# A fused attention and two-MLP kernel: the hidden layer of the first MLP's later part by Strassen's seven block products

## The chip, the cores and the metric

One core of one Trainium2 chip runs the whole program. The metric is the device time of one execution in microseconds (us); the median of several executions counts. The kernel before takes 798.88 us (median of 3 runs, 798.6 to 800.25).

## What is computed

The reference, cut to what matters (attention is left out: it yields x of 2304 tokens and 512 features):

```python
def _moe_ref(x, w_in, w_out, s, b):      # x 2304x512, w_in 512x2048, w_out 2048x512
    h = x @ w_in
    r = np.maximum(h, 0.0)
    g = s * (r * r) + b
    return (g @ w_out).astype(np.float32)

def _moe2_ref(x, w_in, w_out, g_ln):     # w_in 512x1024, w_out 1024x512
    h = x @ w_in
    ...                                  # softmax(h) * h, layer norm, gain g_ln
    return (ln @ w_out).astype(np.float32)
```

The inputs are float64, the result is float32, and all products need nearly float32 accuracy.

## The kernel before, in words

**Products in three terms.** Each operand of the MLPs is split into a high and a low part (F32R, the single-pass float32 form of TensorE). A product is high x high, high x low and low x high, three matmuls into one accumulator in PSUM. In the first MLP the weights are the stationary tile (128 x 128) and the tokens are the moving columns, up to 512 at a time (`NB`); in the second MLP the tokens are stationary.

**Weights.** `order` (line 392) lists all weight tiles: `("in", f)` and `("out", f)` for the 16 chunks of 128 hidden features, then `in2` and `out2` of the second MLP. `decode(n)` (line 441) fetches one as float64 words by a DMA on SP's queue (`fetch`, line 421: 512 KB into one of three `raw` buffers), makes float32 of it with one ScalarE and four VectorE instructions (lines 432 to 438), and splits it into high and low (lines 459, 460). `wpA` and `wpB` hold 28 tiles, and a new one takes the place of an old one. `decode_to` is called from the loops below and so sets how early a tile is made. For `in2`, which is already multiplied by Strassen's scheme, four combinations of blocks are formed on GpSimd (line 451).

**Stages.** Attention (to about 260 us) has the first MLP's first four chunks mixed in (`first_part`), whose partial sums go to DRAM (`yd`). `second_part` (line 952) then does chunks 4 to 15 in ten rounds: two groups of six chunks, and in each group five token blocks, four of 512 tokens and block 3 with 256 (`blocks`, line 840). A round loads x of its block from DRAM (`load2`), splits it (`split2`, `split_x`, lines 798, 799), and for each chunk f calls `hstep` (12 matmuls of `hidden`, lines 769 to 771, into one of two `h` banks, then ReLU, square, scale and split on ScalarE and VectorE, lines 772 to 777) and, one chunk behind, `ystep` (12 matmuls, lines 984 to 986, into the four `y` banks). The end of a round adds the four banks to `yT` (line 1009). `mlp2` (line 1014) does the second MLP; its weights are fetched during `second_part`.

**The order.** `ORDER` writes out the sequence of the instructions of every engine (TensorE, ScalarE, VectorE, GpSimd and SP's DMA issues), by their number in the order in which the program makes them; `SLOTS` the buffer that each tile takes. Each engine issues strictly in this order.

## Time and profile before

| | |
|---|---|
| median of 3 runs | 798.88 us |
| the profiled execution's own time | 798.43 us |
| its span, first to last instruction | 796.7 us |
| TensorE (PE) busy | 788.5 us, 99% |
| VectorE (DVE), ScalarE (ACT) busy | 539.1 us, 545.0 us, 68% each |
| GpSimd (POOL) busy | 111.0 us, 14% |
| DMA | 83.55 MB, 105 GB/s |

The profile is one execution. PE stands for matmuls, PEld for the weight loads that every matmul has and that run beside them, SP for the queue that issues DMAs. Matmuls overlap: a record of a matmul is longer than the time until the next one starts, so that PE's pace is read from the starts. An "idle before" or "waited for" figure names the instruction whose end let the waiting one go.

### The profile page before, as it was taken

The numbers are of one execution on the slowest core, as the hardware profiler recorded it, in microseconds if no ns is written. First come the engines' busy times: TensorE is split into PE (matmuls) and PEld (weight loads), VectorE is DVE, ScalarE is ACT, GpSimd is POOL, SyncE is SP. The second block draws the span as 40 slices with busy tenths as digits, with TensorE's granted clock in tenths as the row PEclk, the third lists the DMA queues.
The fourth block names the chain that finished last, engine by engine and source line by source line (L and its number), as shares of the span: only waits on it lengthen the run. The fifth ranks groups of instructions, "written<-read, shape, count | busy, mean of one in ns | idle before, by whom it ended". The sixth has DMA issues, their size and how long they took to land.

```text
span 796.7 us, 13265 instructions
## 1 busy us (share of the span) xinstructions
PE 788.5 (99%) x4866; PEld 643.6 (81%) x4866; DVE 539.1 (68%) x1329; ACT 545.0 (68%) x1122; POOL 111.0 (14%) x126
## 2 busy tenths in 40 slices
PE   9999999999999999999999999999999999999998
PEld 7777777877777888888888888889888788878886
DVE  6999988988784646455788225355799766665661
ACT  7999998888895558578687575666766444544542
POOL 3222231212101000000001100010112312220110
PEclk9999999999999999999999999999999999999999
DMA  7464764673444353714452130130210001000101
GB/s 259 150 189 126 232 172 139 225 223 113 122 134 128 123 189 96 264 53 135 155 153 88 51 105 1 54 132 1 79 54 1 13 14 41 27 14 14 41 28 53
DMA packets 42005, 83.55 MB, mean 105 GB/s; under 512 B 6652, under 2 KB 17108, under 8 KB 41940
## 3 DMA queue, kind: packets, MB, share of 16 engines
q1 hardware_dynamic: 41940, 82.71, 32.3%
q8 instruction: 38, 0.62, 0.3%
q14 instruction: 27, 0.22, 0.1%
HBM read 68.43 MB, written 14.27 MB: 104 GB/s over the span
## 4 chain that ended last, share of the span: by engine, by line
PE 92%; DVE 5%; ACT 1%; issue 1%; POOL 0%; DVEq 0%; ACTq 0%
PE h L769 9%; PE h L770 8%; PE h L771 8%; PE y L986 6%; PE y L984 6%; PE y L985 6%; PE pp L706 5%; PE s L649 5%; PE po L738 4%; PE o L1118 4%; PE o L1119 4%; PE o L1117 4%; PE y L831 2%; PE zt L1108 2%; PE s L680 2%; PE y L832 2%
## 5 line engine op out<-in xcount | busy, mean ns | idle before, releaser
L769 PE MATMUL h<-xh,w 128*128 128x512 f32 (+1 forms) x320 | 117.1, 379 | 0.0
L770 PE MATMUL h<-xl,w 128*128 128x512 f32 (+1 forms) x320 | 115.4, 373 | 0.0
L771 PE MATMUL h<-xh,w 128*128 128x512 f32 (+1 forms) x320 | 115.0, 373 | 0.0
L772 ACT ACTIVATE r<-h 128x512 f32<-128x512 f32 (+1 forms) x80 | 43.9, 550 | 64.8 <-PE h L771 58.1
L986 PE MATMUL y<-g,w 128*128 128x512 f32 (+1 forms) x240 | 81.9, 369 | 0.0
L985 PE MATMUL y<-g,w 128*128 128x512 f32 (+1 forms) x240 | 81.8, 369 | 0.0
L984 PE MATMUL y<-g,w 128*128 128x512 f32 (+1 forms) x240 | 81.5, 369 | 0.0
L777 DVE TENSOR_TENSOR g<-r,g 128x512 fp32r<-128x512 f32 (+1 forms) x60 | 38.2, 644 | 62.3 <-ACT r L776 62.2
L632 ACT ACTIVATE pr<-pr,mx 128x256 f32<-128x256 f32 (+3 forms) x128 | 71.1, 558 | 4.4 <-DVE mx L665 4.1
L769 PEld LDWEIGHTS h<-xh,w 128*128 128x128 f32 x320 | 59.9, 188 | 13.0 <-ACT r L772 0.5
L710 ACT ACTIVATE pt<-pp,omg 128x256 f32<-128x256 f32 (+3 forms) x128 | 62.6, 524 | 9.9 <-PE pp L706 7.9
L771 PEld LDWEIGHTS h<-xh,w 128*128 128x128 f32 x320 | 59.9, 188 | 10.5 <-issue 0.6
L665 DVE CUSTOM_DVE_ANT_0 pr<-s,big 128x256 f32<-128x256 f32 (+3 forms) x128 | 59.3, 480 | 13.3 <-PE s L649 10.6
L770 PEld LDWEIGHTS h<-xl,w 128*128 128x128 f32 x320 | 59.9, 188 | 10.3 <-issue 0.2
L775 ACT ACTIVATE g<-r,b_sb,s_sb 128x512 fp32r<-128x512 f32 (+1 forms) x60 | 45.6, 768 | 18.5 <-PE y L986 17.8
L1117 PE MATMUL o<-w,zh 128*128 128x512 f32 x144 | 54.9, 394 | 0.0
L1118 PE MATMUL o<-w,zh 128*128 128x512 f32 x144 | 54.2, 391 | 0.0
L1119 PE MATMUL o<-w,zl 128*128 128x512 f32 x144 | 53.8, 390 | 0.0
L986 PEld LDWEIGHTS y<-g,w 128*128 128x128 f32 x240 | 44.7, 188 | 7.7
L985 PEld LDWEIGHTS y<-g,w 128*128 128x128 f32 x240 | 44.4, 188 | 7.3
L706 PE MATMUL pp<-ident,pr 128*128 128x128 f32 x320 | 49.6, 276 | 0.5 <-ACT pt L710 0.5
L984 PEld LDWEIGHTS y<-g,w 128*128 128x128 f32 x240 | 44.2, 189 | 7.1
(177 smaller groups left out, 1840.0 us busy)
## 6 DMA issues: line engine op xcount, KB each, us to landing
raw<-in_moe_w_in_dram SPq DMA_DIRECT2D x24, 512.0 KB, 4.8
raw<-in_moe_w_out_dram SPq DMA_DIRECT2D x24, 512.0 KB, 4.1
kq<-in_kq_dram SPq DMA_DIRECT2D x16, 608.0 KB, 4.2
xr<-xd SPq DMA_DIRECT2D x8, 1024.0 KB, 5.4
RW<-rd SPq DMA_DIRECT2D x24, 288.0 KB, 4.6
q<-in_q_dram SPq DMA_DIRECT2D x16, 320.0 KB, 5.3
v<-in_v_dram SPq DMA_DIRECT2D x16, 320.0 KB, 3.7
xd<-xb SPq DMA_DIRECT2D x4, 1152.0 KB, 6.7
```

The costliest lines, as they stand in the source:

```text
L632: mark[0] = nc.scalar.activation(pr, pr, AF.Exp, bias=mx, scale=-1.0, accum_out=sm).ins
L706: nc.tensor.transpose(pp[:, e * n + c * P:e * n + (c + 1) * P], pr[:, c * P:(c + 1) * P], ident)
L710: nc.scalar.activation(p["pt", i // 2][:, j, 0:i + 1, i % 2, :], pp[:, e * n:(e + 1) * n].rearrange("p (c t) -> p c t", t=P), AF.Copy, sca ...
L769: nc.tensor.matmul(ps, wc[0], xh[:, c, 0:n], start=(c == 0), stop=False)
L770: nc.tensor.matmul(ps, wc[0], xl[:, c, 0:n], start=False, stop=False)
L771: nc.tensor.matmul(ps, wc[1], xh[:, c, 0:n], start=False, stop=(c == NC - 1))
L984: nc.tensor.matmul(o, wc[0], gh[:, 0:n], start=(f == fs[0]), stop=False)
L985: nc.tensor.matmul(o, wc[1], gh[:, 0:n], start=False, stop=False)
L986: nc.tensor.matmul(o, wc[0], gl[:, 0:n], start=False, stop=(f == fs[-1]))
L1117: nc.tensor.matmul(oo, zh, w[:, 0], start=(f == 0), stop=False)
L1118: nc.tensor.matmul(oo, zh, w[:, 1], start=False, stop=False)
L1119: nc.tensor.matmul(oo, zl, w[:, 0], start=False, stop=(f == NF2 - 1))
```

## The change

Chunks f and f + 1 and the two halves of the 512 features form a 2 x 2 block matrix of weights, the two halves of a block's tokens and of the features a 2 x 2 block matrix of x. Instead of eight block products, seven are made, of sums and differences of the blocks (`hidden2`, `product`); each block product has half the tokens as moving columns. The accumulators X, Y, V and W are combined by ScalarE and VectorE (u2, u3, r0, r1), two of them being copied out and then added to by a further product. The seven combinations of x (`forms2`) are made in the first group's rounds, kept in 14 single buffers, also written to DRAM (`fd`), and read back in the second group's rounds. The combinations of weights are made in `decode`; a tile without a free place goes to DRAM (`wd`, `split_w`) and comes back when one is free (`bring`). `wpA` and `wpB` hold 22 tiles; the six half tiles (k = 3) have places of their own. At the start of `second_part` 22 entries of `order` are done, and the rest is spread evenly over the 30 pairs. The y matmuls are the same as before, woven between the products. `ORDER` and `SLOTS` are new; the list of PE grows from 4114 to 4654 entries, that of SP from 205 to 382, VectorE from 1115 to 1272, ScalarE from 941 to 1008, GpSimd from 126 to 170. In the second MLP some buffers are shared with those of `forms2`.

```diff
-    RB = 28 - RA
-    assert 2 * FP2 <= RA + RB
+    RB = 22 - RA
...
-    for f in range(FP1, NF):
-        order += [("in", f), ("out", f)]
+    FH = FP1 + FP2 // 2
+    order += [("out", f) for f in range(FP1, FH)]
+    for f in range(FP1, NF, 2):
+        order += [("win", f, k) for k in range(4)]
+        if f >= FH:
+            order += [("out", f), ("out", f + 1)]
...
+    def bring():
+
+        while staged and room():
+            key, at = staged.pop(0)
+            w = wtiles[key] = place(key)
+            nc.sync.dma_start(w.bitcast(F32), wd[:, at])
 
...
+    def split_w(key, a, sc):
+
+        if key[0] == "win" and key[2] == 3:
+            w = wh.tile([P, 2, WN // 2], F32R, tag="wh", name=f"wh{key[1]}")
+            wtiles[key] = w
+        elif not staged and room():
+            w = wtiles[key] = place(key)
+        else:
+            at = nstaged[0]
+            nstaged[0] += 1
+            staged.append((key, at))
+            w = dec.tile([P, WN, 2], I32, tag="raw", name=f"wt{at}").rearrange("p n t -> p (n t)").bitcast(F32R)
+            w = w.rearrange("p (t n) -> p t n", t=2)
+        if sc is None:
+            nc.scalar.activation(w[:, 0], a, AF.Copy)
+            nc.vector.tensor_tensor(w[:, 1], a, w[:, 0].bitcast(F32), ALU.subtract)
+        else:
+            nc.scalar.activation(w[:, 0], a, AF.Copy, scale=sc)
+            nc.vector.scalar_tensor_tensor(w[:, 1], a, sc, w[:, 0].bitcast(F32), ALU.mult, ALU.subtract)
+        if key not in wtiles:
+            nc.sync.dma_start(wd[:, at], w.bitcast(F32))
+
...
+        if key[0] == "win":
+
+            f, k = key[1:]
+            HN = WN // 2
+            if k == 0:
+                a0, a1 = fetch(n)[0], fetch(n + 1)[0]
+                s1, ss = (dec.tile([P, WN], F32, tag="wa", name=f"{e}{f}", bufs=5) for e in ("s1_", "ss"))
+                s1 = s1[:, 0:HN]
+                a11, a12, a21, a22 = a0[:, 0:HN], a0[:, HN:], a1[:, 0:HN], a1[:, HN:]
+                for o, x, y, op in ((s1, a21, a22, ALU.add), (ss[:, 0:HN], s1, a11, ALU.subtract),
+                                    (a21, a11, a21, ALU.subtract), (ss[:, HN:], a12, ss[:, 0:HN], ALU.subtract)):
+                    nc.gpsimd.tensor_tensor(o, x, y, op)
+                blk["win"] = a0, a1, ss, s1
+            a = blk["win"][k]
...
     def decode_to(n):
         while decoded[0] < min(n, NW):
-            with tc.issue_after(mark[0]) if mark[0] and attended[0] else nullcontext():
-                decode(decoded[0])
+            bring()
+            decode(decoded[0])
...
         n = blocks[rounds[ri][1]][1]
+        m = n // 2
+        tags = ["zh_0", "zl_0", "zh_1", "zl_1", "zh_2", "zl_2"] + [f"f{i}" for i in range(8)]
+        names = "hb11 lb11 hb22 lb22 ht2 lt2 ht3 lt3 ht1 lt1 ht4 lt4 hb21 lb21".split()
+        at = {k: xf.tile([P, KH, NB // 2], F32R, tag=t, name=f"f{k}_{ri}") for k, t in zip(names, tags)}
+        if ri >= len(blocks):
+            for i, k in enumerate("b11 t2 t3 t1 b21 b22 t4".split()):
+                for e in "hl":
+                    nc.sync.dma_start(at[e + k][:, :, 0:m].bitcast(F32), fd[:, names.index(e + k), ri % len(blocks), :, 0:m])
+            return {k[1:]: (at["h" + k[1:]], at["l" + k[1:]]) for k in names if k[0] == "h"}
         x = xq.pop(ri)
-        xh, xl = xsplit(f"2_{ri}")
-        split_x(x[:, :, 0:n], xh[:, :, 0:n], xl[:, :, 0:n])
-        return xh, xl
+        b11, b12, b21, b22 = (x[:, c:c + KH, t:t + m] for c in (0, KH) for t in (0, m))
+        out = {}
+
+        def split(k, b):
+            hi, lo = at["h" + k], at["l" + k]
+            nc.scalar.activation(hi[:, :, 0:m], b, AF.Copy)
+            nc.vector.tensor_tensor(lo[:, :, 0:m], b, hi[:, :, 0:m].bitcast(F32), ALU.subtract)
+            out[k] = hi, lo
+            for e in "hl":
+                nc.sync.dma_start(fd[:, names.index(e + k), ri, :, 0:m], at[e + k][:, :, 0:m].bitcast(F32))
+
+        split("b11", b11)
+        nc.gpsimd.tensor_tensor(b11, b12, b11, ALU.subtract)
+        nc.gpsimd.tensor_tensor(b12, b22, b12, ALU.subtract)
+        split("b22", b22)
+        nc.gpsimd.tensor_tensor(b22, b22, b11, ALU.subtract)
+        split("t2", b22)
+        split("t3", b12)
+        split("t1", b11)
+        split("b21", b21)
+        nc.gpsimd.tensor_tensor(b21, b21, b22, ALU.subtract)
+        split("t4", b21)
+        return out
 
...
+            def product(o, f, k, off, x, more):
+                w = wtiles["win", f, k]
+                xh, xl = xk[x]
+                for i in range(KH):
+                    wc = [w[:, t, off + i * P:off + (i + 1) * P] for t in range(2)]
+                    for z, (a, b) in enumerate(((0, xh), (0, xl), (1, xh))):
+                        nc.tensor.matmul(o, wc[a], b[:, i, 0:m], start=(i == 0 and z == 0 and not more),
+                                         stop=(i == KH - 1 and z == 2), skip_group_check=True)
+
...
+                X, Y = (ps_h.tile([P, 512], F32, tag="h", name=f"{e}_{ri}_{f}")[:, 0:m] for e in "XY")
+                V, W = (p.tile([P, 512], F32, tag=e, name=f"{e}_{ri}_{f}")[:, 0:m] for e, p in (("V", ps_v), ("W", ps_w)))
+                g = []
+                for i in range(2):
+                    g.append(gs.pool.tile([P, 2, NB], F32R, tag=f"g_{gn[0] % 4}", name=f"g2_{ri}_{f + i}", bufs=1))
+                    gn[0] += 1
+                uu = gs.pool.tile([P, 2, NB], F32, tag="g_4", name=f"u{ri}_{f}", bufs=1)
+                u2, u3 = uu[:, 0, 0:m], uu[:, 1, 0:m]
+                r0, r1 = (gs.tile([P, NB], F32, tag="r", name=f"r2_{ri}_{f + i}", bufs=2)[:, 0:n] for i in range(2))
+                HN = WN // 2
+
+                def gate_of(i, r):
+                    gh, gl = g[i][:, 0, 0:n], g[i][:, 1, 0:n]
+                    nc.scalar.activation(r, r, AF.Relu)
+                    nc.scalar.activation(r, r, AF.Square)
+                    nc.scalar.activation(gh, r, AF.Identity, scale=s_sb, bias=b_sb)
+                    mark[0] = nc.scalar.activation(r, r, AF.Identity, scale=s_sb, bias=b_sb).ins
+                    nc.vector.tensor_tensor(gl, r, gh.bitcast(F32), ALU.subtract)
+                    gq[ri, f + i] = (gh, gl, ys, n)
+
+                product(X, f, 0, 0, "b11", False)
+                nc.scalar.activation(u2, X, AF.Copy)
+                yield
+                product(Y, f, 2, 0, "t2", False)
+                nc.vector.tensor_tensor(u2, Y, u2, ALU.add)
+                yield
+                product(V, f, 1, 0, "t3", False)
+                nc.vector.tensor_tensor(u3, V, u2, ALU.add)
+                yield
+                product(W, f, 3, 0, "t1", False)
+                nc.vector.tensor_tensor(r1[:, m:], W, u3, ALU.add)
+                yield
+                product(X, f, 0, HN, "b21", True)
+                nc.scalar.activation(r0[:, 0:m], X, AF.Copy)
+                yield
+                product(W, f, 2, HN, "b22", True)
+                nc.vector.tensor_tensor(r0[:, m:], W, u2, ALU.add)
+                gate_of(0, r0)
+                yield
+                product(V, f, 1, HN, "t4", True)
+                nc.vector.tensor_tensor(r1[:, 0:m], V, u2, ALU.add)
+                gate_of(1, r1)
+                if final:
+                    retire(*(("win", f, k) for k in range(3)))
+                yield
+
...
+            for i, f in enumerate(fs[::2]):
+                decode_to(max(order.index(("win", f, 3)), order.index(("out", f + 1))) + 1)
+                bring()
+                assert ("out", f + 1) in wtiles
+                h = hidden2(f)
+                if i == 0:
+                    weave(h, tails.pop() if tails else iter(()), (0, 0, 1, 1, 2, 2, 2))
+                elif i == 1:
+                    yy = ypair(ri, fs[0])
+                    weave(h, yy, (0, 0, 0, 1, 1, 1, 1))
+                else:
+                    weave(h, yy, (0, 0, 0, 1, 1, 1, 1))
+                    run(yy)
+                    run(ypair(ri, fs[2]))
+                    tails.append(ypair(ri, fs[4]))
                 step += 1
-                if ri == 0:
-                    decode_to(decoded[0] + step % 2)
-                    early = decoded[0]
-                elif ri < len(blocks):
-
-                    decode_to(early + (late - early) * step // steps)
-                elif ri < last:
-
-                    decode_to(late + (last2 - late) * step // steps)
-                else:
-                    decode_to(decoded[0] + 1)
-            if ri == last:
-                decode_to(NW)
-            ystep(fs[-1])
-            for c in range(NC):
-                d = yT[:, c, t0:t0 + n]
-                nc.vector.tensor_tensor(d, ys[c][:, 0:n], d, ALU.add)
-
-    second_part(halves)
+                decode_to(g0 + (NW - g0) * step // steps)
+                bring()
+        run(tails.pop())
+        decode_to(NW)
+        bring()
+        assert not staged
+
```

`product` and `hidden2` stand inside `second_part`; `weave` runs the seven steps of `hidden2` with steps of the y matmuls (12 matmuls of a chunk in four steps) between them, as its list of numbers says.

## Rows read from the trace of the kernel before

**Rows 1.** The page, first part: engine, busy us, share of the span, instructions.

```profile
PE 788.5 (99%) x4866; PEld 643.6 (81%) x4866; DVE 539.1 (68%) x1329; ACT 545.0 (68%) x1122; POOL 111.0 (14%) x126
```

**Rows 2.** The waits of PE, whole span: us in total, times, longest us.

```profile
PE s L649 <- DVE mx L665: 1.1, 2, 0.8
...
PE zt L1108 <- DVE zl L1112: 0.2, 1, 0.2
```

**Rows 3.** Table by stage: us, busy PE, PEld, DVE, ACT, POOL; clock, DMA share, GB/s.

```profile
0.00:299.30 299.30, 296.16 (x2500) 232.52 (x2501) 241.70 (x743) 247.53 (x610) 57.95 (x64) 1.00 0.54 169
299.30:595.00 295.70, 295.70 (x1437) 249.50 (x1436) 169.05 (x300) 203.55 (x347) 17.41 (x16) 1.00 0.29 95
595.00:796.70 201.70, 196.63 (x932) 161.59 (x930) 128.38 (x288) 93.97 (x166) 35.66 (x46) 1.00 0.07 24
...
580.00:620.00 40.00, 39.93 (x184) 32.79 (x183) 37.95 (x80) 24.87 (x43) 8.63 (x11) 1.00 0.07 23
```

**Rows 4.** The timeline of PE, 512 columns: start us, length us, instruction, count.

```profile
425.20 0.39 PE L770 MATMUL h<-xl,w 128*128 128x512 f32 x1
...
431.78 0.39 PE L985 MATMUL y<-g,w 128*128 128x512 f32 x1
```

**Rows 5.** The timeline of PE, 256 columns one after another.

```profile
535.51 0.28 PE L769 MATMUL h<-xh,w 128*128 128x256 f32 x1
...
536.59 0.28 PE L769 MATMUL h<-xh,w 128*128 128x256 f32 x1
```

**Rows 6.** The timeline of PE, transposes of the second MLP, eight in one row.

```profile
621.45 1.07 PE L1108 MATMUL zt<-ident,z 128*128 128x128 f32 x8 [0.35 <-DVE z L1097]
...
```

**Rows 7.** Groups by line and shape, loads and transposes: count | busy us, mean ns | idle before.

```profile
L769 PEld LDWEIGHTS h<-xh,w 128*128 128x128 f32 x320 | 59.9, 188 | 13.0 <-ACT r L772 0.5 <-ACT yo L835 0.4 <-issue 0.4
...
L738 PEld LDWEIGHTS po<-pt,v 128*64 128x64 f32 x384 | 23.0, 137 | 10.0 <-issue 2.8 <-DVE ptl L719 0.4 <-DVE mx L665 0.2
...
L1108 PE MATMUL zt<-ident,z 128*128 128x128 f32 x144 | 19.6, 276 | 1.3 <-DVE sm L1088 0.6 <-DVE z L1097 0.5 <-DVE zl L1112 0.2
```

**Rows 8.** The timeline of PE, 512 and 256 columns mixed, first and last of ten.

```profile
555.58 0.40 PE L769 MATMUL h<-xh,w 128*128 128x512 f32 x1
...
557.11 0.28 PE L986 MATMUL y<-g,w 128*128 128x256 f32 x1
```

**Rows 9.** Groups by line and shape, 299.3 to 595 us.

```profile
L772 ACT ACTIVATE r<-h 128x512 f32<-128x512 f32 x47 | 27.8, 593 | 52.1 <-PE h L771 51.1 <-DVE g L777 0.8
L437 DVE SCALAR_TENSOR_TENSOR raw<-raw 128x512 f32<-128x512 uint32 x30 | 21.7, 734 | 0.2
...
L438 DVE TENSOR_TENSOR wa<-wa,raw 128x512 f32<-128x512 f32 x30 | 20.2, 686 | 0.2
L432 ACT ACTIVATE wa<-raw 128x512 f32<-128x512 f32 x30 | 19.6, 655 | 0.2 <-DVE w L460 0.2
...
L799 DVE TENSOR_TENSOR xl<-xr,xh 128x512 fp32r<-128x512 f32 x28 | 18.8, 687 | 14.4 <-ACT xh L798 14.4
...
L433 DVE TENSOR_SCALAR wa<-wa 128x512 int32<-128x512 int32 x30 | 13.2, 441 | 20.0 <-ACT wa L432 20.0
...
L451 POOL TENSOR_TENSOR wa<-wa,wa 128x512 f32<-128x512 f32 x8 | 10.7, 1332 | 270.5 <-DVE wa L438 262.5 <-DVE w L460 7.7
...
L772 ACT ACTIVATE r<-h 128x256 f32<-128x256 f32 x12 | 4.6, 380 | 4.2 <-DVE g L777 4.2
L1038 POOL TENSOR_TENSOR s<-yT 128x256 f32<-128x256 f32 x4 | 3.4, 852 | 40.5 <-DVE yl L1044 21.9 <-DVE xl L799 18.6
...
L1009 DVE TENSOR_TENSOR yT<-y,yT 128x256 f32<-128x256 f32 x8 | 3.2, 415 | 1.3 <-PE y L986 1.3
```

**Rows 10.** The table by stage, the 20 us of second_part with most DMA.

```profile
320.00:340.00 20.00, 20.00 (x90) 16.56 (x89) 7.89 (x14) 10.63 (x18) 0.00 (x0) 1.00 0.76 263
```

**Rows 11.** DMA issues by line: count, KB each, median us to landing.

```profile
raw<-in_moe_w_in_dram SPq DMA_DIRECT2D x24, 512.0 KB, 4.8
...
yd<-yo SPq DMA_DIRECT2D x16, 256.0 KB, 3.6
```

**Rows 12.** The DMA queue's own waits: us in total, times, longest us.

```profile
SPq L427 <- DVE wa L438: 142.8, 23, 30.6
```

More of the change, by code (lines that the diff above doesn't have):

```diff
@@ L950, in attention_mlp_kernel, with second_part @@
     xs2 = pctx.enter_context(tc.tile_pool(name="xs2", bufs=1, side="right", reuse_waits="tile"))
-    def second_part(halves):
+    ps_v = pctx.enter_context(tc.tile_pool(name="ps_v", bufs=1, space=PSUM, reuse_waits="tile"))
+    def second_part(xk):
         load2(0, True)
         last = len(rounds) - 1
-        g2 = 2 * (FP1 + FG1)
-        late = RA + RB + 2 * FP1
-        last2 = g2 + RA + RB
+        gn = [0]
+        gq = {}
+        tails = []
+        steps = len(rounds) * FG1 // 2
+        step = 0
+        g0 = RA + 8
@@ L958, in second_part @@
         for ri, (fs, bi) in enumerate(rounds):
             t0, n = blocks[bi]
[L960 to L964 removed]
+            m = n // 2
+            final = bi == len(blocks) - 1
+            if ri:
+                xk = forms2(ri)
+            if ri + 1 < len(blocks):
                 load2(ri + 1)
[L966 removed]
@@ new lines, in y2, with ypair, run @@
+                    if f == fs[-1]:
+                        t0 = blocks[bi][0]
+                        d = yT[:, c, t0:t0 + n]
+                        nc.vector.tensor_tensor(d, o, d, ALU.add)
+                    if c == NC - 1 and bi == len(blocks) - 1:
+                        retire(("out", f))
+                    yield
+            def ypair(ri, f):
+                yield from y2(ri, f)
+                yield from y2(ri, f + 1)
+            def run(it, n=99):
+                for _ in range(n):
+                    if next(it, 1):
+                        return
```

171 lines of the change are left out of this document (81 added, 90 removed), and 410 rows, old and new, of the table ORDER.

## The prediction

> **What bounds the kernel now.** I read the page's first part, then the waits of TensorE (PE), then a table by stage, then single matmuls in order of time. PE is busy 99% of the span, and the next engines reach 68% [rows 1]; the waits of PE in the whole run have eight causes, 4.5 us together, the longest single one 1.1 us (first and last of them: [rows 2]). The table by stage [rows 3] cuts the span where the first matmul of second_part (299.3 us) and about where its last one (595 us) stand: in these 295.7 us PE has no idle time at all, while VectorE (DVE) is busy 169 us, ScalarE (ACT) 204 us and the DMA engines 29%. So the stretch that the change rewrites is bound by PE's stream alone, and only what changes that stream, or breaks it, moves the end. "Busy" hides the pace: records overlap. The pace is the distance of starts. With 512 moving columns 30 starts span 425.20 to 431.78, 29 steps of 0.227 us (first and last: [rows 4]). With 256 columns ten starts go from 535.51 to 536.59, 0.120 us a step [rows 5]. PE's clock is 1.00 of full speed in all three stages [rows 3], so no part of the sum is about the clock.
>
> **The change, part by part.**
>
> *Products.* A pair of FF chunks needs today 2 x 12 matmuls over all n tokens of a block; afterwards it needs 7 products x 2 x 3 = 42 matmuls over n/2 tokens. There are 10 rounds with three pairs each. Eight rounds have n = 512, two (block 3, once in each group) have n = 256. Before: 576 x 0.227 + 144 x 0.120 = 130.8 + 17.3 = 148.1 us. After, the 24 full pairs: 24 x 42 = 1008 x 0.120 = 121.0 us, that is 9.8 us less than their 130.8. So a full block gains 7%, not 12.5%: two steps of 0.120 are more than one of 0.227. The six pairs of block 3 are 252 matmuls with 128 moving columns, and no row shows a matmul of this kind (single pass, 128x128 weights, 128 columns). Bounds: the line through 0.227 and 0.120 (0.418 ns a column) gives 0.067 us at 128 columns if columns are all that counts; no less than for 256 columns gives 0.120. Nearest row: the transposes, which stream 128 columns against a 128-row stationary tile, eight in 1.07 us; less the 0.276 of one record, seven steps in 0.79, 0.113 each [rows 6, 7]. They are of another mode, so a second reading: every matmul loads its own weights, and a load record lasts 188 ns with 128 columns, 137 ns with 64 [rows 7]: 51 ns for 64 columns, so about 102 ns for the 128 columns of a load, whatever a load's fixed part is. While 512 or 256 columns stream, a load of that length is hidden; behind 128 columns, which stream in 54 ns, it is not. Both readings stand near the upper end. I take 0.113: 252 x 0.113 = 28.5 us where 17.3 were. Together 121.0 + 28.5 = 149.5 against 148.1: **+1.4 us** (ends: -10.3 at 0.067, +3.1 at 0.120). The gain on the big blocks is spent on the small one.
>
> The Trainium skill, page "TensorE: Matmul & The Clock Gate", section "LDWEIGHTS (loading the stationary operand)", says that a load takes its columns divided by 1.2 ns, 107 ns for 128. By that rule the 252 matmuls would take 27.0 us and this part would come to -0.1 us; the trace's 51 ns for 64 columns agree with it within 5%, but no row shows a load that PE waits for.
>
> *Shorter matmuls between longer ones.* Where 512 and 256 columns alternate, ten starts go from 555.58 to 557.11 [rows 8]: 1.53 us, where four steps of 0.227 and five of 0.120 make 1.51; eight switches, some 3 ns each. Read out of the new order list, h and y matmuls change column count some 520 times from the start of second_part on: **+1.6 us**. The y matmuls and their columns stay as they are.
>
> *PSUM turnover.* h had two banks in turn and one eviction per chunk. Now X and Y use these two and V and W one each; an accumulator is copied out and then continued, so PE's next product into it waits for ACT or DVE. Laid out at the paces above, the new order leaves at least 0.8 us between the last matmul of a product and the next into the same bank (0.7 us once, in a 128-column pair). An ACT eviction of 128x256 takes 380 ns, a DVE one 415 ns [rows 9]; the matmul's own tail is 0.28 - 0.12 = 0.16 us [rows 5]. That fits with 0.2 us to spare, if ACT and DVE are free just then. Today an eviction of 512 columns takes 593 ns [rows 9], and all that PE's loads waited for it is 0.5 us [rows 7].
>
> *ACT and DVE.* Per pair 5 DVE adds (415 ns) and 2 ACT copies (380 ns) are new: 24 full pairs and 6 with half the columns at two thirds of that, 58 us on DVE and 21 us on ACT. The splits of x go from 32 full and 8 half ones to 28 and 7, -3 us each. Fewer weights are ready at 299 us (22 list entries, not 28), so ten more float64 fetches fall into the stretch: on DVE 0.73 + 0.69 + twice 0.44 = 2.3 us each, on ACT 0.66 [rows 9], 23 and 7 us; and some 14 more weight splits, 10 us on each. DVE goes from 169 to about 257 us of 300, ACT from 204 to about 238: 86% and 79%. Both stay below PE, so by themselves they cost nothing; what is lost is the slack that hid a late instruction. GpSimd gets 4 adds for each of the 4.5 x blocks (1.33 us each) and 4 half ones for each of six pairs of weights (0.85 us, both [rows 9]), 44 us of 300.
>
> *DMA.* The stretch moves 95 GB/s x 295.7 us = 28 MB today [rows 3]. New: 14 forms of 262 KB written for 4.5 blocks and read back, 33 MB; no x for the second group, -4.7 MB; ten more fetches, 5 MB; about 23 weights (my count by the list of free places) written and read, 24 MB. 86 MB in 300 us is 285 GB/s. The best 20 us of the stretch move 263 GB/s at a share of 0.76 [rows 10], 346 at a full one, so the share would be about 0.82. A 512 KB fetch lands after 4.8 us, 256 KB after 3.6 [rows 11]. The forms are single buffered: in the second group each is loaded between its last product of one round and its first of the next, 4 to 11 us by the new order, all 3.7 MB within some 20 us. SP issues in order, already waits 143 us for DVE to give raw buffers back [rows 12], and issues 382 instead of 205 instructions; behind a form's load that waits for PE stand the fetches and the staged weights. I put the sum of broken streams at **+1.5 us** (0.15 for each of ten rounds): above nothing, since slack shrinks on three resources, and low, since the new order leaves the gaps named above. Against it, the last fetches no longer crowd the end of the stretch (580 to 620 us: DVE 37.95 of 40 us busy; the last stage has 5.1 us without a matmul [rows 3]), **-0.5 us**.
>
> *Sum.* 1.4 + 1.6 + 1.5 - 0.5 = +4.0. The profiled execution took 798.43 us with a span of 796.7, 1.73 outside it; 800.7 + 1.73 = 802.4. The median shown is 0.45 above that execution: **802.9 us**.
>
> **Rivals.**
> 1. *128 columns run at their own pace* (0.067). Then the change keeps its gain: -10.3 + 1.6 + 1.5 - 0.5 = -7.7, **791.2 us**, faster. It turns at 252 x t = 27.1 - 2.6, t = 0.097. For it: 512 and 256 lie on one line [rows 4, 5]. Against it: [rows 6, 7]. 25%. The skill's same page, section "Back-to-back issue gap", gives about 81 ns for 128 columns in a stream of loads and matmuls; by that estimate the time would be 794.8. No row here shows it.
> 2. *The DMA queue or DVE comes late.* If the queues don't pass the 263 GB/s seen [rows 10], 86 MB need 327 us instead of 300; a late fetch holds ACT, in whose order the copies of X stand, and PE stops. Half of these 27 us gives **816 us**. For it: one queue issuing in order, single-buffered forms, DVE at 86%. Against: the share was never the limit in this stretch. 19%.
> 3. *128 columns are slower still*, like 512: 0.227 x 252 = 57.2 where I have 28.5, **831.6 us**. Nothing in the rows asks for it. 5%.
> 4. *Nothing is late and a load takes 0.102*: 25.7 instead of 28.5 and no broken stream, 4.3 us less than the forecast: **798.6 us**, no change. 9%.
>
> **How the numbers follow.** 0.2% is 1.6 us, about what a measurement of this kernel can tell from no change. My forecast's case has the remaining 42%, 6 of them near enough to the time before to count as no change. Faster: rival 1's 25 and 3 of rival 4's 9, 0.28. Same: the other 6 of rival 4 and the 6, 0.12. Slower: 36, 19 and 5, 0.60. The range 789 to 817 holds rivals 1, 2 and 4 at their prices; it leaves out rival 3 and what lies beyond the price of rival 2; the likeliest case alone lies between 799 and 807.
>
> **What would show it.** PE's matmul count must rise by 540 to 5406. Steps between products: 0.120 in full blocks, 0.10 to 0.12 in block 3; 0.067 there means rival 1. PE idle within second_part under 2 us, or rival 2 with waits of PE for X, V or W's evictions, for forms (fd) or weights (wd), and a DMA share above 0.9. I am wrong if the stretch shrinks below 295 us, or grows past 305.

## The result and the profile after

The changed kernel takes **806.39 us** (median of 4 executions, 805.14 to 807.24); the kernel before takes 798.74 us beside it (4 executions, 798.26 to 800.25). The ratio is 1.0091, with a 95% interval from 1.0072 to 1.0111: 0.9% slower. The profiled execution's span grew from 796.7 to 804.3 us, by 7.6.

The page of the changed kernel, its first part (engine, busy us, share of the span, instructions; before it was [rows 1]):

```profile
PE 794.9 (99%) x5406; PEld 666.4 (83%) x5406; DVE 604.4 (75%) x1486; ACT 567.7 (71%) x1189; POOL 157.0 (20%) x170
```

PE has 540 matmuls more, as foretold, and still fills the span. The other engines gained work, but none became the bound.

The table by stage of the changed kernel, columns as in [rows 3], with the 20 us of most DMA share below it. The cut is at the first product (289.7 us) and behind the last y matmul (601.7 us):

```profile
0.00:289.70 289.70, 286.17 (x2437) 222.50 (x2438) 252.13 (x752) 246.34 (x609) 67.52 (x72) 1.00 0.57 177
289.70:601.70 312.00, 311.27 (x2036) 281.43 (x2035) 223.16 (x445) 225.80 (x411) 55.43 (x52) 1.00 0.72 241
601.70:804.30 202.60, 197.41 (x936) 162.43 (x934) 129.06 (x291) 95.55 (x169) 34.03 (x46) 1.00 0.11 38
...
420.00:440.00 20.00, 20.00 (x141) 18.53 (x140) 15.52 (x34) 18.00 (x32) 3.23 (x4) 1.00 0.89 287
```

In the second stage DVE and ACT are busy 72% each (223 and 226 of 312 us), less than the 86% and 79% of the prediction; DMA runs at a share of 0.72 and 241 GB/s, and single 20 us stretches pass the 263 GB/s of [rows 10].

The middle row (312.0 us) can't be set beside 295.7 us as it stands, since first_part now ends inside it and the second MLP begins inside it. So I added, for each matmul of `second_part`, the distance from its start to the next start. The h (products) and y matmuls of the second part together take **296.8 us before and 303.5 us after: +6.7 of the 7.6 us**. Everything else together makes +0.9. Inside these 303.5 us I call a matmul late where its distance is more than 20 ns above the median of the matmuls with the same columns before, in and behind it. Late time is 0.2 us in 3 places before, and 4.8 us in 45 places after. In rows of equal columns a step is 0.1194 us with 256 columns (mean of 185, before) and 0.1117 with 128 (111, after).

Groups of the changed kernel by line and shape (columns as in [rows 9]): the evictions into u and r, and the gate split.

```profile
L1119 DVE TENSOR_TENSOR g<-r,g 128x512 fp32r<-128x512 f32 x48 | 33.5, 700 | 15.1 <-ACT r L1118 11.4 <-PE V L1098 3.5
...
L1132 DVE TENSOR_TENSOR r<-W,u 128x256 f32<-128x256 f32 x24 | 10.2, 423 | 1.9
L1126 DVE TENSOR_TENSOR u<-Y,u 128x256 f32<-128x256 f32 x24 | 10.1, 422 | 14.9 <-ACT u L1123 13.4 <-PE Y L1098 1.4
...
L1123 ACT ACTIVATE u<-X 128x256 f32<-128x256 f32 x24 | 9.0, 376 | 12.6 <-PE X L1098 6.7 <-DVE r L1138 5.6
```

An eviction takes what was assumed (0.42 for 0.415, 0.376 for 0.380 us). The last column shows who waits for whom: DVE's split for ACT's gate, its copies out of the accumulators for PE, ACT's copy for PE and DVE. These waits cost nothing by themselves; they show that each engine's work hangs on the other two.

The timeline of PE in the changed kernel: first and last of 14 starts with 256 columns; first and last of 14 with 128 columns; three in which 128 and 512 columns alternate.

```profile
362.45 0.28 PE L1098 MATMUL W<-flt,wh 128*128 128x256 f32 x1
...
364.00 0.28 PE L1098 MATMUL X<-fhb,w 128*128 128x256 f32 x1
...
403.83 0.27 PE L1098 MATMUL Y<-flt,w 128*128 128x128 f32 x1
...
405.29 0.27 PE L1098 MATMUL W<-fht,wh 128*128 128x128 f32 x1
...
396.54 0.22 PE L1098 MATMUL X<-flb,w 128*128 128x128 f32 x1
396.60 0.45 PE L1157 MATMUL y<-g,w 128*128 128x512 f32 x1
396.88 0.22 PE L1098 MATMUL X<-fhb,w 128*128 128x128 f32 x1
```

256 columns: 13 steps in 1.55 us, 0.119 each. 128 columns one after another: 13 steps in 1.46 us, **0.112 each**. Where they alternate, the 128 columns take only 0.06, but the 512 columns behind them 0.28 instead of 0.227: together 0.34, the same sum as 0.112 + 0.227. So a matmul that is too short for its successor's weight load doesn't pay itself; the price appears one matmul later.

Where PE is late, the waits of PE name only the two longest in the second part (us in total, times, longest):

```profile
PE Y L1098 <- DVE flt L962: 0.4, 1, 0.4
PE W L1098 <- DVE r L1132: 0.2, 1, 0.2
```

The second is one of a kind: by the semaphore events in the trace, in 27 of the 45 late places, 2.7 of the 4.8 us, it was this instruction of DVE, the first copy out of W (L1132), that released PE's load of weights there. Four places (1.1 us) stand at the splits of one form near 319 us, the others behind other instructions of DVE and ACT; none was released by a DMA. The timeline of ACT, DVE and PE around the second row:

```profile
374.20 0.82 ACT L1118 ACTIVATE r<-r,b_sb,s_sb 128x512 f32<-128x512 f32 x1
...
375.05 0.69 DVE L1119 TENSOR_TENSOR g<-r,g 128x512 fp32r<-128x512 f32 x1 [0.26 <-ACT r L1118]
375.85 0.42 DVE L1132 TENSOR_TENSOR r<-W,u 128x256 f32<-128x256 f32 x1
...
375.51 0.63 PE L1155 MATMUL y<-g,w 128*128 128x512 f32 x2
376.32 0.39 PE L1098 MATMUL W<-fhb,w 128*128 128x256 f32 x1 [0.19 <-DVE r L1132]
376.55 0.40 PE L1155 MATMUL y<-g,w 128*128 128x512 f32 x1
```

DVE waits for ACT's fourth gate instruction, then splits the gate (L1119), and only then copies W out (L1132), because the buffer `r` that it writes is the one the gate is still reading. PE's next product into W should have started two steps of 0.227 behind 375.51, at 375.96, and starts at 376.32. The next step is 0.23, where 256 columns before 512 take 0.12: the second part of the price.

The price is due even when PE's matmul starts on time. Another place, with the weight loads (PEld):

```profile
425.41 0.42 DVE L1132 TENSOR_TENSOR r<-W,u 128x256 f32<-128x256 f32 x1
...
425.65 0.19 PEld L1098 LDWEIGHTS X<-flb,w 128*128 128x128 f32 x1
...
425.76 0.28 PE L1098 MATMUL X<-flb,w 128*128 128x256 f32 x1
425.89 0.19 PEld L1098 LDWEIGHTS W<-fhb,w 128*128 128x128 f32 x1
425.89 0.38 PE L1098 MATMUL W<-fhb,w 128*128 128x256 f32 x1
...
426.11 0.28 PE L1098 MATMUL X<-fhb,w 128*128 128x256 f32 x1
```

Behind 256 columns a load starts 0.12 us ahead of its matmul (425.65 and 425.76). W's load had to wait for DVE and starts with its matmul, which itself is only 0.01 us late; the step behind it is 0.22 instead of 0.12. Of the 4.8 us, 2.1 are late starts (13 places), 1.35 the steps right behind these (13, 0.104 each), and 1.4 steps behind a matmul that was on time with a load that was not (19).

### The profile page after: what moved, and what is told of

The parts are those of the page before. It is cut to its first block, busy times and chain, and to the rows that moved or that the text cites. A ratio compares the mean times of both kernels' runs of the same rounds, so it can differ in the third digit from the quotient of the medians.

```text
span 804.3 us, 15061 instructions
## 1 busy us (share of the span) xinstructions
PE 794.9 (99%) x5406; PEld 666.4 (83%) x5406; DVE 604.4 (75%) x1486; ACT 567.7 (71%) x1189; POOL 157.0 (20%) x170
## 4 chain that ended last, share of the span: by engine, by line
PE 89%; DVE 5%; ACT 3%; issue 1%; DMA 1%; POOL 1%; SPq 0%; DVEq 0%; ACTq 0%; POOLq 0%
PE y L1157 6%; PE y L1156 6%; PE y L1155 6%; PE pp L791 5%; PE W L1098 5%; PE X L1098 5%; PE V L1098 5%; PE s L734 5%; PE po L823 4%; PE o L1308 4%; PE o L1307 4%; PE o L1309 4%; PE Y L1098 2%; PE y L917 2%; PE y L919 2%; PE zt L1298 2%
## 5 line engine op out<-in xcount | busy, mean ns | idle before, releaser
L1155 PE MATMUL y<-g,w 128*128 128x512 f32 (+1 forms) x240 | 84.1, 379 | 0.0
L1156 PE MATMUL y<-g,w 128*128 128x512 f32 (+1 forms) x240 | 83.3, 376 | 0.0
L1157 PE MATMUL y<-g,w 128*128 128x512 f32 (+1 forms) x240 | 81.9, 377 | 0.0
L717 ACT ACTIVATE pr<-pr,mx 128x128 f32<-128x128 f32 (+3 forms) x128 | 71.0, 558 | 4.3 <-DVE mx L750 3.9
L795 ACT ACTIVATE pt<-pp,omg 128x512 f32<-128x512 f32 (+3 forms) x128 | 62.7, 524 | 9.6 <-PE pp L791 8.2
L750 DVE CUSTOM_DVE_ANT_0 pr<-s,big 128x256 f32<-128x256 f32 (+3 forms) x128 | 59.1, 482 | 10.4 <-PE s L734 9.2
L1098 PE MATMUL X<-fhb,w 128*128 128x256 f32 (+1 forms) x240 | 61.8, 277 | 0.0
L1098 PE MATMUL V<-fht,w 128*128 128x256 f32 (+1 forms) x240 | 61.0, 278 | 0.0
L1119 DVE TENSOR_TENSOR g<-r,g 128x512 fp32r<-128x512 f32 (+1 forms) x60 | 39.2, 654 | 22.9 <-ACT r L1118 19.2
L1117 ACT ACTIVATE g<-r,b_sb,s_sb 128x512 fp32r<-128x512 f32 (+1 forms) x60 | 45.8, 767 | 11.7 <-PE y L1157 10.4
L1115 ACT ACTIVATE r<-r 128x512 f32<-128x512 f32 (+1 forms) x60 | 34.5, 582 | 22.9 <-DVE r L1138 13.2
L791 PEld LDWEIGHTS pp<-ident,pr 128*128 128x128 f32 x320 | 37.9, 140 | 13.0 <-ACT pt L795 2.1
L628 POOL TENSOR_TENSOR q<-ph,zb 128x640 f32<-128x640 f32 x16 | 25.7, 1608 | 112.1 <-DVE ph L625 86.3
L1098 PEld LDWEIGHTS X<-fhb,w 128*128 128x128 f32 x240 | 44.3, 190 | 2.8 <-ACT r L1135 0.2
L1118 ACT ACTIVATE r<-r,b_sb,s_sb 128x512 f32<-128x512 f32 (+1 forms) x60 | 45.7, 768 | 1.1
```

The lines of the kernel that those rows point to most:

```text
L717: mark[0] = nc.scalar.activation(pr, pr, AF.Exp, bias=mx, scale=-1.0, accum_out=sm).ins
L750: nc.vector.tensor_tensor_reduce(pr, ss[:, j, at[i]:at[i] + n], big[:, CF * P - i * P:CF * P - i * P + n], -scale, FMAX, ALU.add, ALU.min, mx)
L791: nc.tensor.transpose(pp[:, e * n + c * P:e * n + (c + 1) * P], pr[:, c * P:(c + 1) * P], ident)
L795: nc.scalar.activation(p["pt", i // 2][:, j, 0:i + 1, i % 2, :], pp[:, e * n:(e + 1) * n].rearrange("p (c t) -> p c t", t=P), AF.Copy, sca ...
L1098: nc.tensor.matmul(o, wc[a], b[:, i, 0:m], start=(i == 0 and z == 0 and not more), stop=(i == KH - 1 and z == 2), skip_group_check=True)
L1117: nc.scalar.activation(gh, r, AF.Identity, scale=s_sb, bias=b_sb)
```

## The experiments

A letter for a theory belongs to the text it stands in. A ratio is to the kernel before as it ran beside that run (medians 798.7 to 799.3 us). In the table "h + y" is the sum of the second part's distances as above, from one profile each, and "late" the part of it that is late (places in brackets; in `load96` steps are also told apart by the columns of the weights).

| run | median us (executions) | ratio to before (95%) | h + y us | late us |
|---|---|---|---|---|
| before | 798.74 (4) | | 296.8 | 0.2 (3) |
| changed | 806.39 (4) | 1.0091 (1.0072, 1.0111) | 303.5 | 4.8 (45) |
| load96 | 802.67 (1) | | 300.2 | 5.6 (46) |
| plain3 | 798.60 (10) | 0.9995 (0.9986, 1.0005) | 296.6 | 8.8 (63) |
| nofd | 805.20 (4) | 1.0076 (1.0060, 1.0093) | 303.4 | 4.7 (43) |
| side_first | 806.19 (4) | 1.0093 (1.0069, 1.0117) | 304.4 | 5.7 (28) |
| gate3 | 805.16 (4) | 1.0078 (1.0062, 1.0094) | 301.4 | 3.7 (33) |
| gate3_side_first | 810.21 (4) | 1.0124 (1.0095, 1.0153) | 303.8 | 6.1 (34) |
| gate1 | 804.96 (4) | 1.0076 (1.0057, 1.0095) | 301.5 | 2.9 (25) |
| shift | 808.06 (4) | 1.0109 (1.0091, 1.0126) | 303.6 | 6.0 (51) |
| gate3_pad | 804.15 (4) | 1.0066 (1.0051, 1.0080) | 301.6 | 3.0 (29) |
| plain3_gate3 | 797.10 (10) | 0.9983 (0.9969, 0.9997) | 291.9 | 5.4 (42) |
| plain3_gate3_side_first | 799.16 (10) | 0.9999 (0.9989, 1.0008) | 295.4 | 8.8 (47) |
| plain3_gate3_pad | 796.05 (6) | 0.9966 (0.9953, 0.9978) | 293.6 | 6.1 (39) |

`shift` runs the instructions of the changed kernel in the same order, and its late time differs by 1.1 us; a difference of that size between two profiles says little.

**What a matmul with 128 columns waits for.** In block 3, 228 of the 252 matmuls use 96 of their weights' 128 columns:

```diff
-                        nc.tensor.matmul(o, wc[a], b[:, i, 0:m], ...
+                        r = slice(0, 96 if m == P and (more or i or z) else P)
+                        nc.tensor.matmul(o[r], wc[a][:, r], b[:, i, 0:m], ...
```

> The changed kernel, but in block 3 all matmuls of a product after its first load only the first 96 of the 128 weight columns (the last 32 rows of those accumulators are left short). The moving columns stay 128. Theory A, the weights' load sets the step behind 128 moving columns: the profile of the change shows 0.112 us a step; load records grow by 51 ns from 64 to 128 columns, so 32 columns less are 26 ns less: 0.086 us a step, 228 matmuls, about -6 us (near 800.5). Rival B, a fixed cost of each matmul sets it: 0.112 as before and no change of the time (806.4).

The timeline of PE in this run, two of the matmuls that still load all columns (the first of V and of W) with the short ones between them:

```profile
403.10 0.27 PE L1133 MATMUL V<-fht,w 128*128 128x128 f32 x1
403.21 0.25 PE L1133 MATMUL V<-flt,w 128*96 128x128 f32 x1
403.30 0.33 PE L1133 MATMUL V<-fht,w 128*96 128x128 f32 x2
403.47 0.25 PE L1133 MATMUL V<-flt,w 128*96 128x128 f32 x1
403.55 0.25 PE L1133 MATMUL V<-fht,w 128*96 128x128 f32 x1
403.64 0.27 PE L1133 MATMUL W<-fht,wh 128*128 128x128 f32 x1
403.75 0.25 PE L1133 MATMUL W<-flt,wh 128*96 128x128 f32 x1
```

A step is 0.085 us here (five from 403.21 to 403.64) and still 0.11 from the start of a matmul with a full load. The moving columns are 128 in all of them: the load of the weights sets the pace, 27 ns for 32 columns of weights. The second part fell by 3.3 us, less than 228 x 0.027 = 6.2. Only 151 of the 228 stand behind another matmul with 128 columns and gained (4.1 us); the others, behind longer ones, take 0.06 us in both kernels, and late time rose by 0.8. The time is a single execution.

**Block 3 without the seven products.** Its six pairs form h as before, by four products with 256 columns (144 matmuls for 252); the other blocks are left as changed.

```diff
+                if bi == 3:
+                    X, V, W = (p[0] for p in full)
...
+                    product(X, f, 0, 0, "b11", False, n)
...
+                    product(V, f, 1, 0, "b11", False, n)
...
+                    product(X, f, 0, HN, "b21", True, n)
...
+                    product(W, f, 1, HN, "b21", False, n)
...
```

> The changed kernel, complete, but block 3 is done by four products with 256 moving columns from the same weight tiles (h of f: a11 b1 + a12 b2; h of f+1: a11 b1 - (a11 - a21) b1 + a22 b2), 144 matmuls of 0.119 us instead of 252 of 0.112. Theory A: 17.2 us instead of 28.2, -11 us, 795.5 (794 to 797), so faster than the kernel before by 0.4%. If the 128-column matmuls were only an accident of the order and their time were found again elsewhere, the time would stay within 2 us of 806.4.

798.60 us: the whole loss against the kernel before is gone, and no more than that. That is 3 us above the 795.5 expected. By the steps, 144 x 0.119 = 17.2 for 252 x 0.112 = 28.2 saves 11 us; 6.9 came, because late time rose from 4.8 to 8.8 us. The order of the instructions was written out for the longer stream; that a faster PE meets the same instructions of the other engines earlier would explain the rise, and no run shows it. But it isn't evictions alone: among the waits of PE in the second part of this run are

```profile
PE y L1240 <- DVE g L1175: 0.7, 1, 0.7
...
PE X L1152 <- DMA fhb<-fd: 0.3, 1, 0.3
PE W L1152 <- DMA fht<-fd: 0.3, 1, 0.3
```

Two are for forms on their way back from DRAM, one each. With the steps behind them they are 1.1 us of the 8.8, where the changed kernel has none; the runs built on `plain3` have such waits too.

**Is it the DMA traffic?** No forms are written to DRAM or read from it, 33 MB less; the second group computes with the forms of round 4. (`skip` leaves the places of missing instructions in the written order empty.)

```diff
+        if ri >= len(blocks):
+            skip(tc, "SP", 14)
+            return kept[0]
...
-            for e in "hl":
-                nc.sync.dma_start(fd[:, names.index(e + k), ri, :, 0:m], at[e + k][:, :, 0:m].bitcast(F32))
+            skip(tc, "SP", 2)
```

> The changed kernel without the forms' way through DRAM: forms are not written, and the second group uses the forms of the first group's last round (its operands are wrong, its work on the engines is the same). Some 33 MB less are moved. Rival C: DMA was what made the engines late; PE's waits go, -3 to -5 us (802). Theory A: waits for W stay as they are, the time falls by 1.3 us at most (the one wait for Y near 319 us), 805 to 806.5.

4.7 us of late time against 4.8, and 303.4 us against 303.5. The single-buffered forms and their 33 MB are not what breaks PE's stream in the changed kernel. The staged weights and the fetches are still there. Against them speaks the changed kernel's trace: no late place was released by a DMA, and in the second part ACT waits for a fetch only twice, 2.2 us near 594 us, where nothing is late, and 0.3 us near 495, with 0.16 us of late time behind it.

**W's eviction ahead of the gate split.** It goes to a spare buffer, stands before the gate split where the two were neighbours, and ACT takes the ReLU of that chunk in two halves. (WADDS marks the eviction for the swap in VectorE's order; JOINED gives the second half the place behind the first.)

```diff
-                nc.vector.tensor_tensor(r1[:, m:], W, u3, ALU.add)
+                WADDS.add(nc.vector.tensor_tensor(mtail[:, 0:m], W, u3, ALU.add).ins.name)
...
+                    if aside:
+                        nc.scalar.activation(r[:, m:], mtail[:, 0:m], AF.Relu)
+                        JOINED.add(nc.scalar.activation(r[:, 0:m], r[:, 0:m], AF.Relu).ins.name)
```

> The changed kernel, complete, with W's first eviction going to a buffer of its own (a mask of the attention that is free by then) instead of into r1, and, in VectorE's order, ahead of the gate's split (gl = r - gh) wherever that split stands right before it. ReLU of that chunk becomes two instructions of half the size (about 0.2 us more ScalarE per pair). Theory A (the breaks of PE's stream come from W's eviction queued behind that split, because r1 is still in use): most of the 4.8 us lost in waits of over 20 ns goes, -2.5 to -3.5 us, near 803.4; waits for W fall from some 17 to under 5. Rival C (they come from DMA traffic that makes ScalarE and VectorE late): no change within 1 us.

Late time behind W's first copy fell from 27 places (2.7 us) to 2 (0.15), so the cause of W's wait is shown: the copy's place behind the gate split and the buffer that it shares with it, which this edit changes together. The time did not fall: all the other late time rose from 2.1 us to 5.5. The worst place, in the timelines of GpSimd (POOL), ACT, DVE and PE in this run:

```profile
504.09 0.76 POOL L1266 TENSOR_TENSOR s<-s,yT 128x256 f32<-128x256 f32 x1
504.93 1.07 POOL L1266 TENSOR_TENSOR s<-yT,s 128x256 f32<-128x256 f32 x1
...
504.24 2.30 DVE L1157 TENSOR_TENSOR g<-r,g 128x512 fp32r<-128x512 f32 x2
...
506.63 0.38 ACT L1173 ACTIVATE r<-X 128x256 f32<-128x256 f32 x1 [2.12 <-DVE g L1157]
...
507.07 0.39 PE L1132 MATMUL X<-fhb,w 128*128 128x256 f32 x1 [1.10 <-ACT r L1173]
```

Two gate splits take 2.30 us together, where one takes 0.69: they run beside GpSimd's adds. ACT's copy of X stands behind them, and PE behind the copy. In the changed kernel's second part, ten DVE instructions are longer than the median of their like by over 0.3 us, 5.0 us in sum, and every one of them overlaps an add on GpSimd, six of them one that the change brought; before it was five with 2.8 us, and in this run 16 with 10.4 us. In the changed kernel 0.9 of the 4.8 us late stand within 1.5 us behind the end of such an instruction. Which of the two engines starts first decides who pays. Two places of the changed kernel:

```profile
342.13 0.69 DVE L1119 TENSOR_TENSOR g<-r,g 128x512 fp32r<-128x512 f32 x1
...
342.17 1.25 POOL L534 TENSOR_TENSOR ss<-wa,ss 128x256 f32<-128x256 f32 x1
...
348.11 1.29 POOL L976 TENSOR_TENSOR xr<-xr 128x512 f32<-128x512 f32 x1
...
348.73 1.22 DVE L962 TENSOR_TENSOR flt<-xr,fht 128x512 fp32r<-128x512 f32 x1 [2.08 <-ACT fht L961]
```

In the first, DVE is first and takes its usual 0.69; the add on 256 columns takes 1.25 where its like take 0.74. In the second the add is first and takes 1.29, the shortest of its like; the split takes 1.22 instead of 0.68. In the second part DVE adds and subtractions with both inputs in SBUF overlap a GpSimd instruction by over 0.3 us 22 times: in the 13 where DVE was first, GpSimd's is longer by 0.3 to 0.9 us each time; in the 9 where GpSimd was first, DVE's is longer in 8, by 0.34 to 0.77 us. The copies out of PSUM overlap like this 28 times, and none is longer. No run took GpSimd's adds away, so what they cost PE in sum stays open.

**A shorter gate.** ACT gates a chunk with three instructions instead of four; the square takes the root of s as its scale, and DVE's split adds b. A second run joins this with the edit for W, a third with `plain3`, a fourth with both.

```diff
-                    nc.scalar.activation(r, r, AF.Square)
-                    nc.scalar.activation(gh, r, AF.Identity, scale=s_sb, bias=b_sb)
-                    mark[0] = nc.scalar.activation(r, r, AF.Identity, scale=s_sb, bias=b_sb).ins
-                    nc.vector.tensor_tensor(gl, r, gh.bitcast(F32), ALU.subtract)
+                    nc.scalar.activation(r, r, AF.Square, scale=root)
+                    mark[0] = nc.scalar.activation(gh, r, AF.Identity, bias=b_sb).ins
+                    skip(tc, "Activation", 1)
+                    nc.vector.scalar_tensor_tensor(gl, r, b_sb, gh.bitcast(F32), ALU.add, ALU.subtract)
```

> Second part only: ScalarE's gate of a chunk is three instructions instead of four (the square takes the root of s as its scale, the second Identity is left out, VectorE's gate split adds b itself), as the first part's gate nearly does. The whole result is formed. The fourth instruction takes 0.81 us in the changed kernel's profile (48 full, 12 half ones at 0.60), so ScalarE gets up to 46 us less of 226 in the second part. Theory A, the waits come from ScalarE's and VectorE's instructions standing in line ahead of the accumulators' evictions: PE's waits in the second part fall from 4.8 us to under 2.5, the time from 806.4 to 802.5 to 804.5. Rival B, the evictions are as early as the accumulators allow, and what stands ahead of them is no cause: waits stay at 4.4 to 5.2 us and the time at 805.5 to 807.

> The shorter gate together with the former edit for W (its first eviction goes to another buffer and ahead of the gate split, the ReLU of that chunk in two halves), whole result. Theory A: the former edit moved W's waits to V, X and Y because ScalarE had no room for it; with room the waits fall below 1.5 us in sum and the time to 801.5 to 803.5. Rival B: other accumulators wait again, 4 to 6 us in sum, time 805.5 to 807.

> Four plain products with 256 columns in block 3 (798.6 us, PE's waits in the second part 8.8 us), now with the shorter gate, whole result. Theory A: waits under 5 us, time 793.5 to 796, faster than the kernel before (about 799). Rival B: waits 8 to 9.5 us, time 797.8 to 799.5.

> All three edits together, whole result. Theory A: waits under 3 us, time 791.5 to 794.5. Rival B: waits 8 to 9.5 us, time 797.8 to 799.5.

Only the last text had a theory with both its numbers, rival B for all three edits together (8.8 us late, 799.16 us); the other three runs lie outside both of theirs. Late time fell by 1.1 us alone and by 3.4 together with `plain3`; the edit for W made both worse again. `plain3_gate3` is the first that is faster than the kernel before, by 0.2%. h and y gained 2.1 us in `gate3`, but the time only 1.2: the second MLP, which the edit does not touch, took 204.5 us instead of 202.1, a step of 512 columns 0.231 instead of 0.227. The new tile `root` takes 32 bytes, and by my count of the tiles it moved the gate tiles and part of the weights by as much; the traces show no addresses.

**Is it the address?** In one run `root` takes an unused word beside s, so that nothing moves; in the second the changed kernel gets an unused tile, so that all of this moves and nothing else differs; the third is the gate that moves nothing, with `plain3`.

```diff
-        root = const.tile([P, 1], F32, name="root")
...
-    s_sb = const.tile([P, 1], F32, name="s_sb")
+    s_root = const.tile([P, 2], F32, name="s_root")
+    s_sb, root = s_root[:, 0:1], s_root[:, 1:2]
```

```diff
+        const.tile([P, 1], F32, name="unused")
```

> The shorter gate again, with the root of s in the unused second word beside s, so that no tile of the kernel changes its address; in the run gate3 the new tile had moved the weights and gate tiles by 32 bytes, and in the second MLP 512 columns took 0.231 us a step instead of 0.227, 2.3 us in sum. Whole result. Theory D, the 32 bytes make that: the second MLP takes 202 us again instead of 204.5, the time is 802.5 to 803.5 instead of 805.2. Rival E, it is chance or the program's length: 204.5 again, 805 to 806.

> The changed kernel with one unused 32-byte tile and nothing else (weights and gate tiles 32 bytes further). Whole result. Theory D: the second MLP takes 204.4 us instead of 202.1, the time 808 to 809.5. Rival E: 202 us, 806 to 807.

> Plain products in block 3, the shorter gate, and no tile moved; whole result. Theory D: 794 to 795.5, faster than the kernel before by 0.5%. Rival E: 796.5 to 797.5.

The timeline of PE in the second MLP of the changed kernel, first and last of 20 starts with 512 columns:

```profile
709.07 0.62 PE L1308 MATMUL o<-w,zh 128*128 128x512 f32 x2
...
713.38 0.62 PE L1307 MATMUL o<-w,zh 128*128 128x512 f32 x2
```

And of `shift`, first and last of 16:

```profile
715.74 0.39 PE L1284 MATMUL c<-w,yh 128*128 128x512 f32 x1
...
719.21 0.40 PE L1287 MATMUL d<-w,yl 128*128 128x512 f32 x1
```

19 steps in 4.31 us are 0.227, 15 in 3.47 are 0.231. The second MLP takes 204.4 us in `shift` and 202.1 in `gate3_pad`, each as the theory of the address has it (D). It holds for every run here: 204.4 or 204.5 us in the five with the added tile, 202.0 to 202.2 in the changed kernel and the seven without. The medians moved the same way, 808.06 and 804.15, though `gate3_pad` and `plain3_gate3_pad` came out 0.6 us above what was expected, the latter with more late time (6.1 us) than the profile of `plain3_gate3` (5.4). That an unused tile does it is shown; what about the addresses does it is open.

**The gate almost left out**, ACT with two instructions for it (DVE's split adds b, as in `gate3`; the square and s are missing):

```diff
-                    nc.scalar.activation(r, r, AF.Square)
-                    nc.scalar.activation(gh, r, AF.Identity, scale=s_sb, bias=b_sb)
-                    mark[0] = nc.scalar.activation(r, r, AF.Identity, scale=s_sb, bias=b_sb).ins
...
+                    mark[0] = nc.scalar.activation(gh, r, AF.Identity, bias=b_sb).ins
...
```

> The changed kernel, second part without the square, the scale and the second Identity on ScalarE (two instructions of a gate instead of four; the gate is the ReLU plus b, the square and s are left out). Theory A, instructions standing in line on ScalarE and VectorE make PE's waits: they fall from 4.9 us to under 2, the time to 802 to 803.5 (no more than the 4.9 can come back). Rival B, the accumulators' own turnover makes them: 4.4 to 5.2 us, time 806 to 807.

The page of this run, its first part: ACT has 76 us less than in the changed kernel.

```profile
PE 793.3 (99%) x5406; PEld 666.8 (83%) x5406; DVE 608.3 (76%) x1486; ACT 492.1 (61%) x1069; POOL 156.2 (19%) x170
```

Late time is 2.9 us, no better than with one instruction less (3.0 in `gate3_pad`), and 13 places (1.3 us) are still behind W's first copy. The three runs with the long gate and the same products (changed, `nofd`, `shift`) have 4.7 to 6.0 us, the three with a shorter one (`gate3`, `gate3_pad`, `gate1`) 2.9 to 3.7. So the length of ACT's line costs 1 to 3 us, some 1.9 in the changed kernel. The other 3 stay when ACT has a third instruction less too. That they hang on the order in which DVE and PE have their instructions is a guess: only a new order for all engines would show it, and that was not tried.

**A version faster than both.** `plain3_gate3_pad` takes 796.05 us, 0.9966 of the kernel before (0.9953 to 0.9978). Its page, first part:

```profile
PE 782.9 (99%) x5298; PEld 655.5 (83%) x5298; DVE 604.2 (76%) x1463; ACT 526.7 (66%) x1124; POOL 155.5 (20%) x168
```

It keeps the seven products where they have 256 columns, and 6.1 us of its second part are still late.

## Why the prediction was right, and where it was not

The forecast was 802.9, slower; 806.4 is 3.5 above it, inside the range, and still inside the 799 to 807 of the likeliest case. That it is slower was no luck: products and switches, the two terms that were worked out from rows, measured +2.0 us by themselves. Term by term:

- *Products*, foretold +1.4: right. 252 x 0.1117 + 1008 x 0.1194 = 148.5 us, against 147.8 for the h matmuls before by the steps of both traces: +0.7. The step of 128 columns was put at 0.113, and is 0.112. The reason given, the load of the weights and not the moving columns, is shown by `load96`. (89 of the 252 take only 0.06 us and leave the rest of their price to the next matmul; the sum is nearly the same.) The gain on the big blocks is indeed spent on the small one: `plain3` gives it back.
- *Shorter matmuls between longer ones*, foretold +1.6: right. What is left of h + y without the plain steps and the late time is 2.4 us after and 1.0 before, +1.3.
- *Broken streams*, put at +1.5: **this is the term that failed in size; it measured +4.7** (4.8 late against 0.2, rounded). Two readings behind it went wrong. "That fits with 0.2 us to spare, if ACT and DVE are free just then": the evictions were as long as assumed, but DVE is not free, because W's copy needs an `r` that the previous gate split is still reading, and the gate waits for four instructions on ACT. That accounts for 2.7 of the 4.8 us, and `side_first` shows it. The 0.2 us also had no place for the load of the next weights, which starts 0.12 us ahead of its matmul: where it can't, the step behind is longer by up to 0.11 us, 2.7 us in 32 places (1.35 of them behind a late matmul). And GpSimd's new adds were counted as 44 us that cost nothing; six of DVE's ten prolonged instructions overlap them. The 1.5 itself, 0.15 us for each of ten rounds, rested on no row.
- *The end of the stretch*, put at -0.5: not seen. All that is not h and y of the second part came to +0.9: attention +1.8, the rest of it -0.9. Among the runs with the same attention code that part scatters from 180.2 to 183.2 us, with 179.5 before, so what it is worth stays open.
- *Sum*: +0.7 + 1.3 + 4.7 + 0.9 = +7.6, the growth of the span, for +4.0.

**The rivals.** 1 (128 columns at 0.067) fell: 0.112 is past its turning point of 0.097. 2 named the DMA queue or DVE: for the changed kernel the forms' traffic is cleared by `nofd` and the rest, but for 0.16 us, by the trace, DVE's lateness is real, and the price of 816 is not reached. That single-buffered forms can hold PE, as this rival has it, shows in `plain3`. 3 and 4 fell with the step of 0.112 and the 4.8 us.

The Trainium skill, page "TensorE: Matmul & The Clock Gate", section "LDWEIGHTS (loading the stationary operand)", has 107 ns for 128 columns of weights, and by it, as an estimate, 80 for 96. The steps measured are 112 and 85, so the slope agrees (27 ns for 32 columns), with 5 ns on top. The 81 ns of that page of the Trainium skill, section "Back-to-back issue gap", do not hold for this stream. The Trainium skill, page "SBUF — State Buffer", section "SBUF: two separate sides", says that a DVE instruction with two inputs in SBUF and a GpSimd instruction that reads SBUF exclude each other from a shared pair of ports, and that the one which starts first has the pair for the whole instruction. The trace agrees: GpSimd's is longer in 13 of 13 overlaps with DVE first, DVE's in 8 of 9 with GpSimd first.

**What was to show it.** 5406 matmuls: so. 0.120 in full blocks, 0.10 to 0.12 in block 3: 0.119 and 0.112. A stretch between 295 and 305 us: 303.5 by the sum of steps of h and y (296.8 before); from its first matmul to its last it is 312.0, with other stages' matmuls inside, and can't be judged. PE idle for under 2 us in the second part: late by 4.8, so wrong by that measure; as idle time the waits of PE name only 0.6.

## What to carry to other kernels

Splitting a product into fewer but shorter matmuls pays only while the moving columns last longer than the load of the next weights: here 256 columns do (0.119 against 0.112), and 128 columns cost nearly as much as 256. Before counting an eviction's slack, follow who still reads the buffer that it writes, and which instructions stand ahead of it on its engine; a gap of 0.2 us on PE is none if another engine's whole gate lies in it. Count the load of the next weights into the gap as well: an eviction that ends just in time for the matmul is too late for the load. An edit that adds a tile can move others: keep the addresses when the effect to be measured is below 1%.

## What the runs showed of the hardware that was not expected

- A matmul too short to cover the next load does not pay itself: 128 columns behind 512 take 0.06 us, and the 512 columns behind them 0.28.
- After a wait the step behind it is longer by 0.104 us (13 such steps in the changed kernel), and by up to 0.11 us even where the matmul started on time and only its load had waited (19 steps).
- A DVE gate split of 0.69 us takes 1.0 to 1.7 us where an add on GpSimd had started before it; where the split starts first it keeps 0.69 to 0.84 and the add of 0.74 takes 1.1 to 1.3. Copies out of PSUM keep their 0.42 us beside the same adds.
- One unused tile, which by my count shifts others by 32 bytes, changes the step of 512 columns in the second MLP from 0.227 to 0.231 us, 2.3 us of the time.
